# The eight small products of each weight fold at the highest priority on TensorE, in another order

## The chip, the cores and the metric

The kernel runs on one core of one Trainium2 chip. The metric is the device time of one execution in microseconds (us), the median of several runs. Engines are called as in the profile: PE is TensorE (matmuls), PEld its weight loads, DVE is VectorE, ACT ScalarE, POOL GpSimd, SP SyncE, which issues most DMAs. All arithmetic is in 32-bit floats; a matmul of the program whose operands are plain float32 leaves two MATMUL records in the trace, so that eight small products show as x16.

## The reference

Three stages follow each other. The first is attention by landmarks, for 4 batches (b) of 8 heads with 576 tokens of 64 numbers:

```
A = softmax(q k_lm^T);  Bm = softmax(q_lm k_lm^T);  C = softmax(q_lm k^T)
Z = an approximate inverse of Bm, by 6 steps of  Z = 2 Z - Z Bm Z
attn = A Z C v
```

`q_lm` and `k_lm` are means over blocks of 18 tokens, 32 of them per head. The second and third stage are gated feed-forward layers over the 2304 tokens (width 512):

```
x1 = ((attn w_a) * (attn w_b)) w_out          inner width 1536
x2 = (h * tanh(softplus(h))) w_out2,  h = x1 w_in2     inner width 2048
```

## The kernel before, in words

The attention output is never formed. For each batch the small matrix `Z C v` of all heads is kept as a tile `mt` (128x128, `MT[b]`), and the weights `w_a` and `w_b` are multiplied by it in advance: that is a **fold**. `fold(b, g)` (line 558) takes one sixth `g` of the inner width and issues eight products: for each half `c` of the 128 rows (64 rows each) and each of four strips `j` of 32 output partitions, a product of 64 rows by 32 columns with 512 columns streamed. The strips `j` and halves `c` lie on different parts of PE's array; the result fills `ps_bm`, a pair of PSUM banks (`pair_bank("bm")`, line 82, one buffer only). ACT then copies it to a tile `bm` (the high part), and DVE subtracts that from PSUM (the low part); `bm` has three buffers. There are 4 x 6 = 24 folds. They are numbered here 1 to 24 in their order on PE.

Each `ab` step (line 591) multiplies `bm` by the tile `at` of the attention weights, twice six matmuls of 128x128 with 288 columns into `ps_ab`; ACT and DVE make the gated product `g` of it, POOL its low part. `emit_o1` (line 630) multiplies `g` by the second weights into `ps_o`, twelve matmuls at a time, and ACT or DVE evict it to `x2acc`. Beside this run the attention of later batches (tiles `rz`, `bc`, `ET`, `E`, `kt`, `qt`; many small products of 32x32 or 64x32) and the conversion of the 64-bit input weights to float32 (`to_f32`, line 444: a DMA into one of three `stg` buffers, one ACT and four DVE instructions into `f` or `wab`). The folds of batches 0 and 1 use `wab` tiles straight from that conversion; those of batches 2 and 3 load them back from DRAM (`load_wab`, line 519; three `wab` buffers).

What sets the order: up to the end of a list written by hand (`ORDER_1`, issued at line 840) the instructions of PE, ACT and DVE are held in the order in which the program writes them; folds 1 to 4 lie there. From then on a scheduler draws up each engine's order beforehand: of the instructions that its own model of time takes to be ready it puts the one with the highest priority first, and priority otherwise follows the order in which the program wrote them. SP's DMAs are ordered in this way too. On the chip each engine then works through its own list strictly in order and waits by semaphores. The last third of the program (the third stage) is again mostly held.

Of the kernel before, what the change touches and what calls it, by code (L numbers as in the profile page):

```python
# [31 lines left out]
def nystrom_moe_kernel(ctx: ExitStack, tc: tile.TileContext, q, k, v, w_a, w_b, w_out1, w_in2, w_out2, q1, k1, out):  # L32
# [49 lines left out]
    def pair_bank(tag):  # L82
        return two.get(tag, ps).tile([128, 2, 512], F32, tag=tag, bufs=1, name=f"ps_{tag}")
# [473 lines left out]

    def fold(b, g):
        p = pair_bank("bm")
        for c in range(2):  # L560
            r = slice(64 * c, 64 * c + 64)
            for j in range(4):
                pe.matmul(
                    p[32 * j:32 * j + 32, c], MT[b][r, 32 * j:32 * j + 32],
                    wab[g][r, j].rearrange("p a f -> p (a f)"), start=True, stop=True,
                )
        t = main.tile([128, 2, 2, 512], F32R, tag="bm", bufs=3, name="bm")
        yield
        ac.activation(t[:, 0], p, AF.Copy)
        yield  # L570
        ve.tensor_tensor(t[:, 1], p, t[:, 0].bitcast(F32), op=ALU.subtract)
        bm[b, g] = t

    def emit_bm(b, g):
        for _ in fold(b, g):
            pass
# [239 lines left out]
    for n in range(N_UNITS):  # L816
        part[f"c{n}"] = unit(n)
    part["f0"], part["f1"], part["F0"], part["F1"] = fold(0, 0), fold(0, 1), fold(1, 0), fold(1, 1)
    for n in range(N_SLOTS):
        b, m = divmod(n, 8)  # L820
# [343 lines left out]
```

## Time and profile before

| what | value |
|---|---|
| median of 3 runs | 831.23 us (830.99 to 831.99) |
| profiled execution, own time | 834.0 us |
| its span in the trace | 832.2 us |
| PE busy | 797.8 us, 96% of the span |
| DVE busy | 541.7 us, 65% |
| ACT busy | 361.1 us, 43% |
| chain that ended last | PE 78%, DVE 8%, DMA 7%, ACT 3% |

Busy time is the union of an engine's instructions. Matmuls are pipelined and a record is longer than the distance to the next start, so what an instruction or a group costs PE is read as the distance from its start to the next group's start. All folds lie in the first half, between 35 and 405 us.

### The profile page before, as it was taken

To read this page: it belongs to the slowest core of one execution; us is meant where nothing else is said; L and a number is where in the kernel's file an instruction comes from. 1 tells how busy PE (TensorE), PEld (TensorE's weight loads), DVE (VectorE), ACT (ScalarE), POOL (GpSimd) and SP (SyncE) were. 2 spreads that over 40 slices of the span, in tenths; PEclk is the share of its full clock that TensorE was granted. 3 is DMA by queue.
4 is the path that set the end of the run, shared out by engine and by line. 5 is a ranking of instruction groups with operands and counts; after the bars stand their busy time and mean duration, and the time that the engine had idled before them with its cause. 6 is when DMAs were issued, how large, how long until landed. Compare 5 with 4: busy or idle time off the path is not lost.

```text
span 832.2 us, 14803 instructions
## 1 busy us (share of the span) xinstructions
PE 797.8 (96%) x5854; PEld 689.5 (83%) x5854; DVE 541.7 (65%) x1012; ACT 361.1 (43%) x824; POOL 141.9 (17%) x143
## 2 busy tenths in 40 slices
PE   5869999999999999999999999999999999999998
PEld 3356778997787887888889889988999999899997
DVE  7868887895498498886796765768433447433433
ACT  3645845444334344454353543554332335332332
POOL 1011212222141242222221344330000000000000
PEclk9889999999999999999999999999999999999999
DMA  9977466558527748868324887878645545555502
GB/s 353 293 280 257 149 233 219 194 179 285 184 68 250 290 143 300 283 209 292 108 93 133 324 335 276 303 280 344 215 179 237 217 185 232 215 192 224 191 0 76
DMA packets 48732, 183.44 MB, mean 220 GB/s; under 512 B 4260, under 2 KB 12452, under 8 KB 39320
## 3 DMA queue, kind: packets, MB, share of 16 engines
q1 hardware_dynamic: 39832, 169.40, 57.1%
q10 hardware_dynamic: 8832, 13.11, 4.3%
q8 instruction: 46, 0.75, 0.4%
q14 instruction: 22, 0.18, 0.1%
HBM read 129.02 MB, written 53.48 MB: 219 GB/s over the span
## 4 chain that ended last, share of the span: by engine, by line
PE 78%; DVE 8%; DMA 7%; ACT 3%; issue 3%; SPq 1%; ACTq 0%; POOL 0%; DVEq 0%
PE ps_ab L56 35%; PE ps_o L56 22%; PE ps_bm L56 12%; PE ps_at L56 10%; DMA tok<-in_k_dram 2%; DMA kt<-in_k_dram 2%; DVE f L56 2%; DMA vt<-in_v_dram 1%; DMA stg<-in_moe_w_a_dram 1%; DMA stg<-in_moe_w_out_dram 1%; ACT sa L56 1%; DVE wab L56 1%; DVE bm L56 1%; DVE tg L56 1%; DVE s L56 1%
## 5 line engine op out<-in xcount | busy, mean ns | idle before, releaser
L56 PE MATMUL ps_ab<-xc,wc 128*128 128x384 f32 x1008 | 197.1, 336 | 1.2 <-DVE u2s L56 1.0
L56 PE MATMUL ps_ab<-at,bm 128*128 128x288 f32 x1152 | 186.6, 302 | 4.7 <-DVE tg L56 3.5
L56 PEld LDWEIGHTS ps_ab<-xc,wc 128*128 128x128 f32 x1008 | 178.5, 188 | 12.5 <-DVE u2s L56 1.4
L56 PEld LDWEIGHTS ps_ab<-at,bm 128*128 128x128 f32 x1152 | 160.9, 189 | 30.2 <-issue 9.2
L56 PE MATMUL ps_o<-g,wo 128*128 128x288 f32 x1152 | 180.1, 299 | 3.7 <-ACT x2acc L56 3.0
L56 PEld LDWEIGHTS ps_o<-g,wo 128*128 128x128 f32 x1152 | 161.7, 190 | 18.4 <-issue 5.5
L608 POOL TENSOR_TENSOR g<-tg,g 128x288 fp32r<-128x288 f32 x96 | 88.7, 925 | 337.6 <-ACT g L56 274.2
L56 ACT ACTIVATE m<-c 128x384 f32<-128x384 f32 x95 | 49.6, 522 | 176.6 <-DVE c L56 174.5
L56 PE MATMUL ps_bm<-wo,g 128*128 128x512 f32 x288 | 92.8, 391 | 0.0
L56 DVE TENSOR_TENSOR g<-m,g 128x384 fp32r<-128x384 f32 x96 | 62.2, 650 | 30.5 <-ACT g L56 30.0
L56 PE MATMUL ps_at<-wo,g 128*128 128x512 f32 x288 | 81.5, 391 | 0.0
L56 PE MATMUL ps_o<-wo,g 128*128 128x512 f32 x288 | 78.7, 390 | 0.0
L56 DVE SCALAR_TENSOR_TENSOR f<-stg,f 128x512 uint32<-128x512 uint32 x88 | 69.8, 796 | 1.4
L56 ACT ACTIVATE g<-tg 128x288 fp32r<-128x288 f32 x96 | 42.4, 441 | 58.1 <-DVE tg L56 57.4
L56 ACT ACTIVATE ta<-ps_ab 128x288 f32<-128x288 f32 x96 | 38.9, 406 | 63.1 <-PE ps_ab L56 60.1
L56 PEld LDWEIGHTS ps_at<-wo,g 128*128 128x128 f32 x288 | 54.0, 188 | 10.2
L56 DVE TENSOR_TENSOR tg<-ps_ab,ta 128x288 f32<-128x288 f32 x96 | 43.3, 451 | 28.9 <-PE ps_ab L56 22.5
L56 PEld LDWEIGHTS ps_o<-wo,g 128*128 128x128 f32 x288 | 53.6, 188 | 8.7
L56 PEld LDWEIGHTS ps_bm<-wo,g 128*128 128x128 f32 x288 | 53.4, 188 | 6.3
L56 ACT ACTIVATE g<-m 128x384 fp32r<-128x384 f32 x96 | 50.4, 525 | 3.0
L56 DVE TENSOR_TENSOR u2s<-ps_ab,m 128x384 f32<-128x384 f32 x24 | 13.4, 557 | 57.9 <-PE ps_ab L56 57.9
L56 DVE TENSOR_TENSOR c<-ps_ab,m 128x384 f32<-128x384 f32 x23 | 12.8, 558 | 48.6 <-PE ps_ab L56 48.6
(156 smaller groups left out, 803.4 us busy)
## 6 DMA issues: line engine op xcount, KB each, us to landing
wc<-wcd SPq DMA_DIRECT2D x16, 1792.0 KB, 7.4
wo<-wod SPq DMA_DIRECT2D x16, 1024.0 KB, 9.5
stg<-in_moe_w_out_dram SPq DMA_DIRECT2D x28, 512.0 KB, 5.1
wcd<-wc SPq DMA_DIRECT2D x8, 1792.0 KB, 10.6
wab<-wabd SPq DMA_DIRECT2D x10, 1024.0 KB, 7.5
stg<-in_moe_w_in_dram SPq DMA_DIRECT2D x16, 512.0 KB, 6.0
wod<-wo SPq DMA_DIRECT2D x8, 1024.0 KB, 8.4
stg<-in_moe_w_a_dram SPq DMA_DIRECT2D x12, 512.0 KB, 7.4
```

The lines of the kernel that those rows point to most:

```text
L56: i = f(*a, **kw)
L608: gp.tensor_tensor(t[:, 1], tg, t[:, 0].bitcast(F32), op=ALU.subtract)
```

## The change

Inside `fold` the eight products are now traced in a block that gives them the highest priority, and within each half `c` the strips `j` come in the order 3, 2, 1, 0 instead of 0, 1, 2, 3. The products, their operands and their places on the array are the same. The eviction by ACT and DVE keeps its priority.

```
     def fold(b, g):
         p = pair_bank("bm")
-        for c in range(2):
-            r = slice(64 * c, 64 * c + 64)
-            for j in range(4):
+        with tc.high_priority():
+            for c, j in ((c, j) for c in range(2) for j in (3, 2, 1, 0)):
+                r = slice(64 * c, 64 * c + 64)
                 pe.matmul(
                     p[32 * j:32 * j + 32, c], MT[b][r, 32 * j:32 * j + 32],
                     wab[g][r, j].rearrange("p a f -> p (a f)"), start=True, stop=True,
                 )
```

In the order before, 14 folds stand as one group of eight on PE and 10 (folds 5, 6, 9, 11, 12, 17, 18, 21, 23 and 24) in 25 pieces, 39 groups in all; now all 24 stand as one group of eight. Three places of PE's order follow. In them `ps_bm<-wab,mt` are a fold's products, `ps_ab` those of an `ab` step, `ps_o_<n>` those of `emit_o1`, `ps_at<-rz` and `ps_at<-ident,E` small products of the next batch's attention.

The first place, before: fold 11 of batch 1 on PE, at 197 to 208 us of the trace, in four pieces (3, 1, 1 and, behind the rows shown, 3 products).

```order
L56 MATMUL ps_bm<-wab,mt 32x512 x3
L56 MATMUL ps_at<-ident,E 128x128 x4
L56 MATMUL ps_at<-ident,E 64x128
L56 MATMUL ps_bm<-wab,mt 32x512
L56 MATMUL ps_ab<-at,bm 128x288 x12
L56 MATMUL ps_o_2713<-g_2569,wo_2374 128x288
L56 MATMUL ps_o_2758<-g_2459,wo_2181 128x288
L56 MATMUL ps_o_2713<-g_2569,wo_2374 128x288 x2
L56 MATMUL ps_o_2758<-g_2459,wo_2181 128x288 x2
L56 MATMUL ps_o_2758<-g_2526,wo_2181 128x288 x3
L56 MATMUL ps_o_2758<-g_2569,wo_2374 128x288 x3
L56 MATMUL ps_bm<-wab,mt 32x512
```

The same place now, folds 11 and 12:

```order
L56 MATMUL ps_bm<-wab,mt 32x512 x8
L56 MATMUL ps_ab<-at,bm 128x288 x8
L56 MATMUL ps_at<-rz 32x64 x8
L56 MATMUL ps_o_2713<-g_2459,wo_2181 128x288 x3
L56 MATMUL ps_o_2713<-g_2526,wo_2181 128x288 x3
L56 MATMUL ps_o_2758<-g_2459,wo_2181 128x288 x3
L56 MATMUL ps_o_2758<-g_2526,wo_2181 128x288 x3
L56 MATMUL ps_ab<-at,bm 128x288 x6
L56 MATMUL ps_bm<-wab,mt 32x512 x8
L56 MATMUL ps_ab<-at,bm 128x288 x3
```

Fold 11 has moved forward by 22 other matmuls (counted to its first piece) and is whole; fold 12, whose three pieces stood 86 to 176 matmuls behind fold 11's first piece, stands 34 behind fold 11.

The second place, before: fold 18 on PE, at 322 to 326 us of the trace.

```order
L56 MATMUL ps_o_4259<-g_4050,wo_3808 128x288 x3
L56 MATMUL ps_o_4259<-g_4094,wo_3808 128x288 x3
L56 MATMUL ps_bm<-wab,mt 32x512 x5
L56 MATMUL ps_ab<-at,bm 128x288 x6
L56 MATMUL ps_bm<-wab,mt 32x512 x3
L56 MATMUL ps_o_4315<-g_4130,wo_3669 128x288 x3
```

The same place now:

```order
L56 MATMUL ps_o_4259<-g_4050,wo_3808 128x288
L56 MATMUL ps_o_4259<-g_4094,wo_3808 128x288 x2
L56 MATMUL ps_bm<-wab,mt 32x512 x8
L56 MATMUL ps_ab<-at,bm 128x288 x6
L56 MATMUL ps_o_4259<-g_4094,wo_3808 128x288
L56 MATMUL ps_o_4315<-g_4130,wo_3669 128x288 x3
```

Fold 18 stands where its first piece stood; the second piece behind the six products of `ps_ab` is gone.

The third place, before: the matmuls ahead of fold 20 on PE, the last nine rows of the sixty matmuls between folds 19 and 20.

```order
L56 MATMUL ps_o_4405<-g_4275,wo_3808 128x288 x3
L56 MATMUL ps_o_4449<-g_4130,wo_3669 128x288 x3
L56 MATMUL ps_o_4449<-g_4175,wo_3669 128x288 x3
L56 MATMUL ps_o_4449<-g_4231,wo_3808 128x288 x3
L56 MATMUL ps_o_4449<-g_4275,wo_3808 128x288 x3
L56 MATMUL ps_ab<-at,bm 128x288 x12
L56 MATMUL ps_o_4493<-g_4331,wo_3161 128x288 x3
L56 MATMUL ps_o_4493<-g_4375,wo_3161 128x288 x3
L56 MATMUL ps_bm<-wab,mt 32x512 x8
```

The same place now, from fold 19 to fold 20:

```order
L56 MATMUL ps_bm<-wab,mt 32x512 x8
L56 MATMUL ps_ab<-at,bm 128x288 x12
L56 MATMUL ps_o_4315<-g_4275,wo_3808 128x288 x3
L56 MATMUL ps_o_4359<-g_4275,wo_3808 128x288 x3
L56 MATMUL ps_ab<-at,bm 128x288 x6
L56 MATMUL ps_o_4405<-g_4130,wo_3669 128x288 x3
L56 MATMUL ps_o_4405<-g_4175,wo_3669 128x288 x3
L56 MATMUL ps_o_4405<-g_4231,wo_3808 128x288 x3
L56 MATMUL ps_o_4405<-g_4275,wo_3808 128x288 x3
L56 MATMUL ps_bm<-wab,mt 32x512 x8
```

Fold 20 now follows fold 19 after 36 matmuls instead of 60.

Elsewhere the scheduler's order of the other instructions changes too, on PE, DVE, ACT and SP, from about fold 10 on: small products of the attention and `ab` or `emit_o1` groups swap places, and two loads of `wab` on SP's queue (for folds 14 and 15) stand ahead of a load of `stg` and of the next `kt`.

## Rows read from the trace of the kernel before

**Rows 1.** The page: busy time by engine; shares of the chain that ended last.

```profile
PE 797.8 (96%) x5854; PEld 689.5 (83%) x5854; DVE 541.7 (65%) x1012; ACT 361.1 (43%) x824; POOL 141.9 (17%) x143
...
PE 78%; DVE 8%; DMA 7%; ACT 3%; issue 3%; SPq 1%; ACTq 0%; POOL 0%; DVEq 0%
```

**Rows 2.** Groups by line: a fold's products and ACT's eviction (count | busy, mean ns).

```profile
L56 PE MATMUL ps_bm<-wab,mt 64*32 64x512 f32 x384 | 42.0, 608 | 0.2 <-DVE bm L56 0.2
...
L56 ACT ACTIVATE bm<-ps_bm 128x1024 fp32r<-128x1024 f32 x24 | 24.5, 1023 | 19.9 <-PE ps_bm L56 18.7 <-PE ps_ab L56 1.2
```

**Rows 3.** Timeline of PE around fold 10: start, duration, line, tiles, count.

```profile
186.38 0.96 PE L56 MATMUL ps_ab<-at,bm 128*128 128x288 f32 x6
187.17 0.42 PE L56 MATMUL ps_o<-g,wo 128*128 128x288 f32 x2
...
189.32 1.09 PE L56 MATMUL ps_bm<-wab,mt 64*32 64x512 f32 x16
190.34 1.06 PE L56 MATMUL ps_ab<-at,bm 128*128 128x288 f32 x6
```

**Rows 4.** Timeline of PE, a single product of fold 11.

```profile
199.12 1.04 PE L56 MATMUL ps_bm<-wab,mt 64*32 64x512 f32 x2
200.10 1.86 PE L56 MATMUL ps_ab<-at,bm 128*128 128x288 f32 x12
```

**Rows 5.** Timeline of PE, fold 18: the six matmuls between its pieces, and the second piece.

```profile
323.91 1.06 PE L56 MATMUL ps_ab<-at,bm 128*128 128x288 f32 x6
324.91 1.06 PE L56 MATMUL ps_bm<-wab,mt 64*32 64x512 f32 x6
325.89 0.66 PE L56 MATMUL ps_o<-g,wo 128*128 128x288 f32 x3
```

**Rows 6.** Folds alone by stretch: length, PE busy, PEld busy, ACT busy, PEclk, DMA.

```profile
97.00:130.00 33.00, 5.34 (x48) 0.80 (x48) 0.00 (x0) 1.00 0.65 224
130.00:189.00 59.00, 3.21 (x32) 0.49 (x32) 0.00 (x0) 1.00 0.57 190
189.00:225.00 36.00, 8.44 (x48) 1.18 (x48) 0.00 (x0) 1.00 0.67 229
...
310.00:327.00 17.00, 5.29 (x32) 0.74 (x32) 0.00 (x0) 1.00 0.77 266
...
347.00:410.00 63.00, 8.50 (x64) 1.24 (x64) 0.00 (x0) 1.00 0.64 220
```

**Rows 7.** All work by stretch: length, PE, PEld, DVE, ACT, POOL busy, PEclk, DMA.

```profile
130.00:189.00 59.00, 59.00 (x490) 53.94 (x492) 49.55 (x98) 26.95 (x60) 14.96 (x18) 1.00 0.57 190
189.00:225.00 36.00, 36.00 (x394) 26.30 (x387) 17.38 (x42) 12.14 (x27) 7.18 (x8) 1.00 0.67 229
...
310.00:327.00 17.00, 17.00 (x118) 11.99 (x117) 13.83 (x23) 7.31 (x14) 5.39 (x5) 1.00 0.77 266
...
347.00:410.00 63.00, 62.49 (x457) 53.64 (x458) 48.48 (x86) 28.05 (x59) 14.78 (x16) 1.00 0.64 220
```

**Rows 8.** Chain in order of time, 95 to 135 us: its two longest pieces.

```profile
100.64 8.44 DMA stg<-in_moe_w_a_dram
...
117.20 8.28 DMA stg<-in_moe_w_out_dram
```

**Rows 9.** Chain between 327 and 347 us, shares by line.

```profile
by line: DVE f L56 29.1%; issue 18.2%; DVE bm L56 10.3%; ACT f L451 9.2%; DVE f L455 7.3%; DVE x2acc L56 6.0%; DVE tg L56 5.2%; ACTq L620 5.0%; POOL g L608 4.1%; ACT g L56 2.2%; PE ps_ab L56 2.1%; PE ps_o L56 2.0%; DVEq L56 0.2%; DVEq L455 
```

**Rows 10.** Chain between 408 and 425 us, shares by line.

```profile
by line: DVE f L56 22.8%; issue 20.4%; PE ps_ab L56 11.8%; DVE xq L56 10.0%; DVE wc L56 6.0%; DVE tg L56 5.3%; DVE f L455 5.0%; ACT f L451 4.3%; ACT wc L56 3.7%; DVE xc L56 3.3%; DVE bm L56 3.0%; ACT g L56 2.6%; DVE x2acc L56 1.3%; ACTq L62
```

**Rows 11.** What PE's matmuls waited for between 97 and 410 us: total, times, longest.

```profile
PE ps_ab L56 <- DVE tg L56: 1.4, 2, 0.9
PE ps_o L56 <- ACT x2acc L56: 1.2, 1, 1.2
```

**Rows 12.** Timelines of PE and DVE: fold 19 and the end of its eviction.

```profile
330.84 1.09 PE L56 MATMUL ps_bm<-wab,mt 64*32 64x512 f32 x16
...
338.49 1.21 DVE L56 TENSOR_TENSOR bm<-ps_bm,bm 128x1024 fp32r<-128x1024 f32 x1
```

## The prediction

> **What bounds the kernel now.** I read the page first, then the same thing by stretch, because a mean over the span mixes stages. PE's matmuls fill 96% of the span and the chain that ended last is 78% PE [rows 1]. All folds lie before 405 us, so the folds alone by stretch came next [rows 6], then all engines in the same stretches [rows 7], then PE's timeline around single folds [rows 3 to 5], and last who ends PE's waits and where the chain leaves PE [rows 8 to 11]. The reader is to see three things. First, a fold is tiny work that takes real PE time: 42.0 us in all [rows 2]. Second, its price goes by the group and not by the product (next part). Third, PE has hardly a wait between 97 and 410 us: the two longest entries are 1.4 and 1.2 us [rows 11]. In the stretches from 130 to 225 us PE's row is full while DVE is busy 49.55 of 59 us and then only 17.38 of 36 [rows 7]. There PE time that goes is time that goes. In two places it is not so. Between 97 and 130 us the chain sits in two weight loads of 8.44 and 8.28 us [rows 8], half of that stretch. Between 327 and 347 us [rows 9], and again between 408 and 425 us [rows 10], it runs through DVE's and ACT's conversion of weights (`f`), with PE at a few per cent of it in the first case. PE's granted clock is at its upper level (1.00) in all these stretches [rows 6, 7], and since the work is the same I leave the clock out.
>
> **The change, part by part.**
>
> *The pieces that go.* A whole fold, eight products, costs PE 190.34 - 189.32 = 1.02 us from its start to the next group's [rows 3]. One product alone costs 200.10 - 199.12 = 0.98 us [rows 4], three cost 325.89 - 324.91 = 0.98 us [rows 5]. The eight evidently run side by side, and a piece pays for a whole fold. Ten folds stand in 25 pieces and now stand in 10: 15 pieces go. Beside this each group of small products costs at its turns: six `ab` matmuls take 187.17 - 186.38 = 0.79 us among their like [rows 3] and 324.91 - 323.91 = 1.00 us between two pieces [rows 5], so 0.21 us for the two turns. A piece that goes gives back its 0.98 us, less some 0.01 by which the piece that takes over its products grows (1.02 for eight against 0.98 for one to three), and 0.2 for its turns: about 1.17 us, and 15 of them 17.5 us.
>
> As a check, by busy time [rows 6]: the five stretches hold 5.34 + 3.21 + 8.44 + 5.29 + 8.50 = 30.8 us for 14 folds (3, 2, 3, 2 and 4 of them). At 1.09 us [rows 3] for each, whole, they would hold 15.3, so 15.5 us go; 0.06 us per piece of this overlaps the next group (1.04 against 0.98 [rows 4]), 0.9 in all, and with 15 x 0.2 for the turns it is 17.6 again.
>
> *What comes back.* The order now puts fold 10 inside a group of 32x32 products, splits a group of landmark products in two, and a pair of `zd` products likewise. No row shows these; by the nearest rows each costs between nothing and a piece with its turns (1.17). I take about a third, 1.0 us for the three together, and keep 0 to 3.5 for the range.
>
> *What of it is on the path, by stretch.* The pieces that go are 2, 1, 5, 3 and 4 in the five stretches (from the orders; [rows 6] agree).
> - 97 to 130 us, 2 pieces, 2.3 us: nothing. The two loads [rows 8] start when DVE has emptied a staging buffer, and PE already waits behind them. PE only waits longer.
> - 130 to 189, 1 piece, 1.2 us: DVE is at 49.55 of 59 us. I take half, 0.6.
> - 189 to 225, 5 pieces, 5.8 us less the 1.0 that comes back: 4.8. DVE is half idle, the path is PE, and what follows moves forward as a whole. The two `wab` loads that move ahead of `kt` on SP wait for folds 11 and 12, which now come earlier, so they do not hold the queue longer.
> - 310 to 327, 3 pieces, 3.5 us: directly behind them the chain is DVE's [rows 9]. DVE is busy 13.83 of 17 us [rows 7], so it can follow by 3.2 at the very most. I take 1.0.
> - 347 to 410, 4 pieces, 4.7 us: DVE is at 48.48 of 63 us and PE is the path, but at its end the chain goes over to DVE and ACT [rows 10]. I take 3.0.
>
> The sum is 0 + 0.6 + 4.8 + 1.0 + 3.0 = 9.4 us. What is late next in each case is DVE, with the conversion of the second weights.
>
> *The start order 3, 2, 1, 0* changes no cost: the eight run together in 1.02 us. Bounds: nothing, to a few start distances per fold, (1.02 - 0.98) x 24 = 1.0 us.
>
> *The eviction* (ACT 1023 ns [rows 2], then DVE 1.21 us [rows 12]) is the same 24 times; it moves with its fold.
>
> Against the profiled execution: 834.0 (span 832.2 and 1.8 around it) - 9.4 = 824.6 us. That execution is 2.8 us over the median of 831.23, so in medians 831.2 - 9.4 = **822 us**.
>
> **A rule weighed.** In the stretch 189 to 225 us PE's matmul row is full, its weight loads fill 26.30 of 36 us, in the stretch before 53.94 of 59 [rows 7]. The Trainium skill (Perfetto Trace Analysis, Identifying the Most-Contended Engine) says that matmul busy time is a poor measure of PE's headroom and that weight-load busy time is to be taken. By it the stretch could be packed to the same 91%, 26.30 / 0.914 = 28.8 us, an estimate of 7.2 us saved where I count 4.8. The trace bears out the direction (the folds hold 8.44 us of matmuls there and 1.18 us of weight loads [rows 6]), but the three whole folds that stay need 3.3 us, so I keep my figure.
>
> **The rivals.**
>
> *All of it arrives.* If DVE and ACT follow PE in every stretch after 130 us, 13 x 1.17 - 1.0 = 14.2 us go: 817. For it: DVE's idle time in the stretches 310 to 327 and 347 to 410 us is 17.7 us [rows 7]. Against: the chain there [rows 9, 10].
>
> *Nothing arrives.* The gain is a longer wait of PE for DVE's conversions: 831. For it: DVE at 84% in 130 to 189 and 81% in 310 to 327 [rows 7], and a new order of everything else that may cost the rest. Against: the five pieces in 189 to 225 us, where DVE has half its time free.
>
> *Slower: a fold at the head of PE's list that waits for its bank.* There is one `ps_bm`, and a fold can start when DVE has evicted the one before. Fold 20 now comes 36 matmuls after fold 19, 36 x 0.79 / 6 = 4.7 us, and with two turns 4.9. In the trace before, fold 19 ended at 330.84 + 1.02 = 331.86 and its eviction at 338.49 + 1.21 = 339.70, 7.8 us later [rows 12]; at that pace PE would stand 2.9 us at fold 20, with everything behind it. Folds 11, 12 and 19 (37, 34 and 31 matmuls after the one before) stand as close. If all four wait 2.9 us and no other gain is lost, 9.4 - 11.6 = -2.2: 833.4. It decides from 9.4 / 4 = 2.4 us of wait at each, that is evictions that end some 7 us after their fold. Against: with ACT and DVE free, an eviction needs 2.2 us, and in 189 to 225 they are mostly free.
> The Trainium skill (TensorE: Matmul & The Clock Gate, Part 2, Step-by-step) says that matmuls stay in program order and only weight loads are pulled ahead, so such a fold would indeed hold all matmuls behind it. No row before shows a long case of it.
>
> **How the numbers follow.** Forecast (part of it arrives, 818 to 828): 0.62. All of it (814 to 818): 0.17. Nothing (829.6 to 832.9): 0.09. Slower (833 to 837): 0.12. A measurement of this kernel can tell 0.2%, 1.7 us, from no change. So faster is 0.62 + 0.17 and a little of the third case's lower edge, 0.80; same 0.08; slower 0.12. The range that holds eight in ten reaches from 814 (all 17.5 us, the first stretch's too) to 831 (nothing); the likeliest case's own range is 818 to 828.
>
> **What would show it.** 24 rows of a fold in PE's timeline, all x16, and PE busy for folds near 24 x 1.09 = 26 us in place of 42.0: the first step. The six `ab` matmuls beside folds near 0.9. By stretch: PE reaches the 12th fold's place some 5 us earlier and the distance holds to fold 16; between the 17th and the 20th fold it hardly grows; PE's waits between 97 and 410 us grow: the two entries of 2.6 us together [rows 11] become 7 us or more, most of it for DVE. The prediction is wrong if `PE ps_bm <- DVE bm` becomes a wait of several us (slower), if waits do not rise (all of it), or if a fold of eight costs clearly more than 1.02 us.

## The result, and the profile after

The changed kernel takes 819.41 us (median of 4 runs, 818.69 to 821.62); the kernel before took 831.25 us beside it (830.99 to 831.99). The ratio is 0.9858 with an interval of 0.9839 to 0.9876, so 11.8 us went. A second comparison of the same two kernels, on another occasion, gave 818.71 against 832.71 us: 0.9829 (0.9806 to 0.9852), 14.0 us. Beside e1 to e3 below, two executions of the kernel before took 1543 and 2680 us; times and ratios there go by its other executions, whose median is 832.2 us. The profiled execution of the changed kernel took 819.76 us with a span of 818.0.

The page of the changed kernel, busy time by engine and the shares of the chain that ended last, answers to [rows 1]:

```profile
PE 779.9 (95%) x5854; PEld 686.8 (84%) x5854; DVE 541.6 (66%) x1012; ACT 359.5 (44%) x824; POOL 139.1 (17%) x143
...
PE 79%; DVE 9%; DMA 5%; ACT 4%; issue 2%; POOL 0%; ACTq 0%; SPq 0%; DVEq 0%
```

The work is the same (5854 matmuls, DVE's busy time alike), and PE is busy 797.8 - 779.9 = 17.9 us less. The groups by line of the changed kernel (count | busy, mean ns) answer to [rows 2]:

```profile
L56 PE MATMUL ps_bm<-wab,mt 64*32 64x512 f32 x384 | 26.1, 600 | 0.5 <-DVE bm L56 0.5
```

42.0 us of busy time for folds became 26.1. PE's timeline of the changed kernel around folds 11 and 12 (start, duration, line, tiles, count), which answers to [rows 3, 4]:

```profile
194.11 1.09 PE L56 MATMUL ps_bm<-wab,mt 64*32 64x512 f32 x16
195.13 1.34 PE L56 MATMUL ps_ab<-at,bm 128*128 128x288 f32 x8
...
199.32 1.09 PE L56 MATMUL ps_bm<-wab,mt 64*32 64x512 f32 x16
```

Every fold is one row of x16, and takes 195.13 - 194.11 = 1.02 us to the next start, what a whole fold took before.

Where the time came from is read between two landmarks, since the time up to fold 7 differs from execution to execution by some 3 us (fold 7 starts between 121.8 and 125.3 us in all profiles of this study but e8's, where it starts at 130.4). One cause shows in the two profiles of the changed kernel: fold 5 starts at 100.75 and 100.74 us, but between 109 and 112.4 us, right behind a wait of PE of about 2 us in both, the granted clock was 0.67 on average in the first and stayed at its upper level, 1.00, in the second, and fold 7 starts 1.9 us later in the first. The landmarks are the start of fold 7 and the first product of the third stage. From the second landmark to the last product of that kind it is 374.4 us in both kernels: the third stage neither gained nor lost. The view of one tile has it for the kernel before (count: shortest/median/longest ns, first to last start; form):

```profile
L56 PE MATMUL ps_ab<-xc,wc x1008: 331/336/445, 446.9 to 821.3; 128*128 128x384 f32 x168
```

and for the changed kernel:

```profile
L56 PE MATMUL ps_ab<-xc,wc x1008: 331/336/444, 432.7 to 807.1; 128*128 128x384 f32 x168
```

Fold 7 itself in PE's timeline, before:

```profile
124.55 1.09 PE L56 MATMUL ps_bm<-wab,mt 64*32 64x512 f32 x16 [0.17 <-DVE bm L56]
```

and after:

```profile
124.54 1.09 PE L56 MATMUL ps_bm<-wab,mt 64*32 64x512 f32 x16 [0.47 <-DVE bm L56]
```

The distance fell from 446.9 - 124.55 = 322.3 to 308.1 us, by 14.2. Two further executions give 321.4 for the kernel before and 309.0 for the changed one. By sections, against the second execution of the kernel before, and with a fold in several pieces taken at the start of its last piece: fold 7 to 9 (one piece less) -1.2 us, 9 to 10 +0.1, 10 to 13 (five pieces) -4.3, 13 to 16 +0.1, 16 to 17 -2.3, 17 to the third stage -5.6 (these last two hold seven pieces): -13.3. Fold 7 itself hardly came earlier, though two pieces had gone ahead of it: it starts at 124.55 and 123.22 us in the two profiles before and at 124.54 and 122.61 after.

How much of this is PE's own work is read in the windows view between the two landmarks (length, PE, PEld, DVE, ACT, POOL busy, PEclk, DMA). Before:

```profile
124.55:446.86 322.31, 317.29 (x2806) 272.35 (x2807) 247.72 (x476) 141.91 (x302) 83.50 (x90) 1.00 0.60 207
```

and after:

```profile
124.54:432.68 308.14, 303.58 (x2806) 270.72 (x2807) 246.88 (x476) 140.81 (x302) 79.88 (x90) 1.00 0.61 212
```

PE is busy 317.29 - 303.58 = 13.7 us less, and stands idle 5.0 us before and 4.6 after. All that PE saved here is time saved.

What lets 310 to 410 us shrink is seen in the same view, taken over windows that hold as many instructions. Before:

```profile
310.00:410.00 100.00, 99.14 (x733) 82.98 (x732) 78.65 (x137) 43.18 (x89) 25.09 (x26) 1.00 0.72 246
```

After:

```profile
303.00:395.00 92.00, 90.65 (x732) 81.50 (x731) 78.13 (x137) 42.22 (x89) 23.63 (x27) 1.00 0.76 259
```

137 DVE instructions and 733 (732) matmuls take 92 us in place of 100; the granted clock is 1.00 in both. DVE is busy 85% in place of 79%. What DVE waited for on PE's account in these two windows (total, times, longest), before:

```profile
DVE tg L56 <- PE ps_ab L56: 6.9, 8, 1.7
DVE xt L56 <- PE ps_bm L56: 2.3, 1, 2.3
DVE x2acc L56 <- PE ps_o L56: 1.5, 2, 1.3
```

and after:

```profile
DVE tg L56 <- PE ps_ab L56: 3.3, 5, 1.3
DVE tg L56 <- PE ps_o L56: 1.4, 1, 1.4
```

Before, DVE stood 6.9 + 2.3 + 1.5 = 10.7 us waiting for PE; after, 4.7. So DVE, which the prediction had as the next limit here, was itself kept waiting by PE.

The chain needs a second execution to be read. In the first profile of the kernel before it is 29.1% DVE's `f` between 327 and 347 us [rows 9]. In the second profile of the same kernel (b_again below) fold 19 stands 1.7 us earlier, and the shares by line at the same place, 325 to 345 us, are all PE's:

```profile
by line: PE ps_o L56 46.0%; PE ps_ab L56 44.7%; PE ps_bm L56 10.2%
```

Two paths of nearly the same length evidently lie side by side there, and [rows 9] shows the one that came last by a little in one execution. In the changed kernel the chain at this place is mostly PE's too. Its shares by line between 320 and 345 us:

```profile
by line: PE ps_ab L56 40.6%; PE ps_o L56 33.9%; DVE f L56 9.3%; PE ps_bm L56 4.1%; ACT bm L56 4.1%; issue 3.5%; DVE f L455 1.5%; ACTq L620 1.4%; ACT ta L56 1.2%; ACT f L451 0.3%; DVE tg L56 0.3%; ACTq L451 0.1%
```

Between 408 and 425 us the chain is DVE's in both profiles of the kernel before ([rows 10], and 28.0% `f` in the second). There it did turn to PE. Its shares between 394 and 411 us, after:

```profile
by line: PE ps_ab L56 45.5%; PE ps_o L56 22.6%; DVE f L56 10.2%; issue 9.8%; ACT wc L56 5.4%; ACT ta L56 4.3%; ACTq L620 1.9%; DVE x2acc L56 0.4%; DVE tg L56 0.4%; DVEq L56 0.3%; ACT f L451 0.2%; ACTq L451 0.1%; ACTq L56 0.1%
```

### The profile page after: what moved, and what is told of

Read it like the earlier page. It is cut to its first block, busy times and chain, and to the rows that moved or that the text cites. A ratio compares the mean times of both kernels' runs of the same rounds, so it can differ in the third digit from the quotient of the medians.

```text
span 818.0 us, 14799 instructions
## 1 busy us (share of the span) xinstructions
PE 779.9 (95%) x5854; PEld 686.8 (84%) x5854; DVE 541.6 (66%) x1012; ACT 359.5 (44%) x824; POOL 139.1 (17%) x143
## 4 chain that ended last, share of the span: by engine, by line
PE 79%; DVE 9%; DMA 5%; ACT 4%; issue 2%; POOL 0%; ACTq 0%; SPq 0%; DVEq 0%
PE ps_ab L56 36%; PE ps_o L56 23%; PE ps_at L56 10%; PE ps_bm L56 10%; DMA kt<-in_k_dram 2%; DVE f L56 2%; ACT sa L56 1%; DVE wab L56 1%; DMA stg<-in_moe_w_a_dram 1%; DMA stg<-in_moe_w_out_dram 1%; DVE bm L56 1%; DVE s L56 1%; DMA s_in<-wi2d 1%; DVE xt L56 1%; DVE f L455 0%
## 5 line engine op out<-in xcount | busy, mean ns | idle before, releaser
L608 POOL TENSOR_TENSOR g<-tg,g 128x288 fp32r<-128x288 f32 x96 | 86.5, 901 | 325.7 <-ACT g L56 314.4
```

The lines of the kernel that those rows point to most:

```text
L608: gp.tensor_tensor(t[:, 1], tg, t[:, 0].bitcast(F32), op=ALU.subtract)
```

## The experiments

Ratios are to the kernel before, run beside each. "Distance" is that from fold 7 to the third stage in the run's own profile.

| run | time (us) | ratio (interval) | groups of fold products | distance (us) |
|---|---|---|---|---|
| before / b_again | 831.25 / 831.66 (one run) | 1 | 39 | 322.3 / 321.4 |
| the change / c_after_again | 819.41 / 818.71 | 0.9858 / 0.9829 | 24 | 308.1 / 309.0 |
| e1_only_5_6 | 832.33 | 1.0000 (0.9988 to 1.0012) | 37 | 322.2 |
| e2_only_9_12 | 827.07 | 0.9938 (0.9918 to 0.9958) | 33 | 315.9 |
| e3_only_17_24 | 823.95 | 0.9903 (0.9886 to 0.9921) | 32 | 314.1 |
| e4_not_5_6 | 818.36 | 0.9831 (0.9807 to 0.9854) | 26 | 307.3 |
| e5_priority_alone | 825.52 | 0.9912 (0.9890 to 0.9934) | 27 | 312.3 |
| e6_order_alone | 825.90 | 0.9930 (0.9909 to 0.9950) | 30 | 315.4 |
| e7_extra_first | 824.17 | 0.9893 (0.9869 to 0.9917) | 24 + 24 | 313.3 |
| e8_extra_between | 845.63 | 1.0137 (1.0099 to 1.0176) | 48 + 24 | 328.8 |
| e9_evict_too | 820.93 | 0.9850 (0.9830 to 0.9871) | 24 | 309.3 |
| e10_landmarks_too | 817.60 | 0.9816 (0.9799 to 0.9833) | 24 | 307.3 |

**A second look at the kernel before** (no edit):

> The kernel before, unchanged, profiled a second time, because its first profiled execution (834.0 us) lay 2.8 us over its median. Theory A (the early stretch, bound by weight loads, varies from execution to execution): this one ends near 831.2 us, and fold 7 starts about 2.5 us earlier than the 124.55 us of the first, while from fold 7 to the end nothing differs by more than 0.5 us. Rival B: the 2.8 us are spread over the whole span, and fold 7 starts within 0.8 us of 124.55.

831.66 us; fold 7 stood at 123.22 us in place of 124.55, and the distance was 0.9 us shorter. Neither theory holds as stated: of the 2.3 us by which the span is shorter, 1.3 lie ahead of fold 7 and 0.9 behind it. This last is the size below which a difference between two profiles says nothing here.

**The change for some folds only** (e1 to e4). The folds are counted as the program writes them; those in `FIRST` get the change, the others stay as before:

```
-        with tc.high_priority():
-            for c, j in ((c, j) for c in range(2) for j in (3, 2, 1, 0)):
+        folds[0] += 1
+        with tc.high_priority() if folds[0] in FIRST else nullcontext():
+            for c, j in ((c, j) for c in range(2) for j in ((3, 2, 1, 0) if folds[0] in FIRST else (0, 1, 2, 3))):
```

e1, `FIRST = (5, 6)`, the two pieces between 97 and 130 us:

> Only folds 5 and 6 are made whole (2 pieces go, between 97 and 130 us); the order of DVE, POOL and SP is that of the kernel before. My theory (that stretch is bound by two weight loads, PE only waits longer): no change, 831.2 us within 0.7. Rival (a piece is worth its 1.17 us of PE time wherever it stands): 828.9 us.

832.33 us against 832.2. Folds 5 and 6 stand whole, and the time does not move: the interval of 1.0000 is 1.0 us to either side, and the rival asked for 2.3. Two pieces there are worth nothing that can be told.

e2, `FIRST = range(9, 13)`, the six pieces between 130 and 225 us:

> Only folds 9 to 12 are whole (6 pieces go, between 150 and 225 us). Prediction's credits: 0.6 + 4.8 = 5.4 us, so 825.8. If every piece after 130 us arrives at 1.17 us: 7.0 less up to 1.0 for split groups of other products, 824.2 to 825.2. If the gain came from the new order of everything else in the later part and not from these pieces: 830 to 831.5.

0.62% of 832.2 is 5.2 us, with an interval of 3.5 to 6.8; the distance fell by 5.5 to 6.4. That rules out the third case, but not one of the first two.

e3, `FIRST = range(17, 25)`, the seven pieces between 310 and 410 us:

> Only folds 17 to 24 are whole (7 pieces go, between 310 and 405 us). Prediction's credits: 1.0 + 3.0 = 4.0 us, so 827.2, because DVE's weight conversion takes over as the bound there. If every piece arrives at 1.17 us: 8.2 us, so 823.0. In the profile the first would show waits of PE for DVE or ACT between 310 and 425 us grow by about 4 us, the second would show them the same.

0.97% of 832.2 is 8.1 us, with an interval of 6.6 to 9.5; the distance fell by 7.3 to 8.2. Seven pieces at 1.17 are 8.2, and the 4.0 of the prediction's credits is ruled out. PE's waits for DVE and ACT between 310 and 425 us are 2.0 us here against 1.2 before: they hardly grew, as the second case asks. Together e2 and e3 give 13.3 us, what the sections of the profile give too, so the two parts add up.

e4, all folds but 5 and 6:

> The changed kernel with folds 5 and 6 in two pieces each as before; all else stands as in the changed kernel. My theory (the stretch from 97 to 130 us is bound by two weight loads): as the changed kernel, 819.4 us within 0.8. Rival (a piece costs 1.17 us anywhere): 821.7 us.

818.36 us, 0.2 us below the range of the theory and 3.3 below the rival; the ratio is 0.9831 against 0.9858 and 0.9829 for the whole change. It is the counterpart of e1.

**Priority alone** (e5), the strips in their old order:

```
-            for c, j in ((c, j) for c in range(2) for j in (3, 2, 1, 0)):
+            for c, j in ((c, j) for c in range(2) for j in (0, 1, 2, 3)):
```

> The priority alone, with strips in the order 0, 1, 2, 3: folds 5, 6 and 9 stand in two pieces, all others whole (27 groups; the change has 24, before 39). If groups set the time and those before 130 us are free: one piece more than the changed kernel, 819.4 + 1.2 = 820.6 us. If the order of strips itself mattered to PE: a fold of eight would take clearly more or less than 1.02 us from its start to the next group.

A miss, by some 5 us: 825.52. Only folds 5, 6 and 9 are split, so one extra piece stands on the path, yet the distance is 312.3, 4.2 us over the change's, and the third stage is 1.8 us longer (435.9 to 812.1, 376.2 us). The scheduler's order of everything else is another. What PE waited for between 300 and 470 us, in this run (total, times, longest):

```profile
PE ps_ab L56 <- DVE tg L56: 2.9, 5, 1.0
PE ps_bm L56 <- DVE g L56: 1.4, 1, 1.4
PE ps_o L56 <- ACT g L56: 0.9, 1, 0.9
PE ps_o L56 <- DVE x2acc L56: 0.7, 2, 0.5
```

and in the changed kernel:

```profile
PE ps_ab L56 <- ACT ta L56: 2.5, 4, 1.4
PE ps_o L56 <- POOL g L608: 0.4, 1, 0.4
```

These are 5.9 us against 2.9, so about 3 of the 5 us are seen as waits of another order; the one of 1.4 us for `g` lies in the third stage. PE's own work is the other part: between the landmarks it is busy 305.96 us against 303.58 in the change, 2.4 us more, of which the one split has 1.1 to 1.2 by e6. Why the order of the strips leads to that order of the rest was not settled.

**Order alone** (e6), no priority:

```
-        with tc.high_priority():
+        if True:
```

> The order of strips alone (3, 2, 1, 0), without the priority: 30 groups, of which 6 are extra pieces and all of these lie after 130 us. If the number of groups after 130 us sets the time: 819.4 + 6 x 1.17 = 826.4 us, or less by what was lost in the last stretches (prediction's credits: 823 to 825). If the early place of a fold (its priority), not its being whole, gave the gain: 829 to 832 us.

A hit: 825.90, and an early place alone is ruled out as the cause of the gain, since 5.8 us of it came without the priority. Six pieces more than in the change stand behind 130 us, and the distance is 6.4 to 7.3 us over the change's, 1.1 to 1.2 a piece.

**The price of splitting a group, by itself** (e7 and e8). Each fold gets one more product, 128x128 with 32 columns, whose result is not used. In e7 it stands ahead of the eight, in e8 between the first four and the last four:

```
+                if (c, j) == (0, 3):      # e7; in e8: (1, 3)
+                    pe.matmul(p[:, 1, 0:32], ident, ident[:, 0:32], start=True, stop=True)
```

> The changed kernel with one more small product per fold, 128x128 with 32 columns, ahead of the eight, into a part of the bank that they overwrite (a product without use). Folds stay whole. By the nearest rows such a product costs PE about 0.1 us, 24 of them 2.4 us at most: 819.4 to 822 us.

> The same extra product, but between the first four and the last four products of each fold, so that every fold is two pieces (48 groups) with everything else as in the run before it. If a piece costs its own 0.97 us and 0.2 us for turns: 17 folds lie after 130 us, so 17 x 1.17 = 19.9 us more than with the extra product ahead, 839 to 842 us. If the gain came from the folds' early place or the new order of the rest, and pieces were nearly free: within 3 us of it.

PE's timeline of e7, the extra product and the fold behind it:

```profile
193.78 0.30 PE L56 MATMUL ps_bm<-ident 128*128 128x32 f32 x2
194.01 1.09 PE L56 MATMUL ps_bm<-wab,mt 64*32 64x512 f32 x16
```

and of e8:

```profile
196.66 1.06 PE L56 MATMUL ps_bm<-wab,mt 64*32 64x512 f32 x8
197.65 0.41 PE L56 MATMUL ps_bm<-ident 128*128 128x32 f32 x2
197.99 1.06 PE L56 MATMUL ps_bm<-wab,mt 64*32 64x512 f32 x8
198.98 0.26 PE L56 MATMUL ps_at<-bc 32*32 32x32 f32 x6
```

Same instructions, another place: four products take 197.65 - 196.66 = 0.99 us, the other four 0.99 us, where the eight together took 1.02. The kernels differ by 1.0137 - 0.9893 = 2.44% of 833.41, 20.3 us for 24 more groups. That splitting alone costs time is shown by this: the rival allowed 3 us.

The size is another matter. The expectation reached nearly this sum, 19.9 us, by 17 folds behind 130 us alone; the time itself, 845.63, lies above its 839 to 842. The windows view between the landmarks, where 18 folds lie, counted from fold 7, has for e7:

```profile
121.77:435.05 313.28, 305.90 (x2841) 275.03 (x2841) 246.98 (x476) 140.53 (x302) 83.09 (x90) 1.00 0.61 213
```

and for e8:

```profile
130.36:459.18 328.82, 326.05 (x2843) 278.35 (x2843) 248.45 (x476) 141.57 (x302) 81.97 (x90) 1.00 0.58 203
```

PE's busy time grew by 326.05 - 305.90 = 20.2 us, 1.12 for each of 18 splits, close to the 1.17 foretold; but PE's idle time fell from 7.4 to 2.8 us, so only 15.5 us arrived, 0.86 each. The rest of the difference of the two profiles lies ahead of fold 7, which starts 8.6 us later in e8, and is in part the clock. Between 64 and 76 us the granted clock was 1.00 in e7 and at its lower level in e8, where PE had been busy 0.88 of the 2 us from 60 to 62:

```profile
64.00:76.00 12.00, 12.00 (x102) 7.11 (x94) 5.98 (x13) 3.32 (x8) 0.00 (x0) 0.50 0.62 226
```

Folds 3 to 6 then stand 6.9 to 7.2 us later than in e7, so the splits between them cost next to nothing there, as in e1. That the total came near 17 x 1.17 is luck.

e7 itself came out above its expectation of 822 at most: 24 times the extra product's 0.23 us is 5.5, and 0.9893 is 0.35% or 0.64% over the change's two ratios, 2.9 or 5.3 us. The scheduler's order is not the change's throughout: fold 17 starts 178.1 us after fold 7 in e7, 183.7 in the change, and at folds 5, 6, 9 and 17 other matmuls stand between the extra product and the eight. So this is no clean price of the product.

**The eviction too** (e9): ACT's and DVE's instruction of a fold also at the highest priority.

```
-        ac.activation(t[:, 0], p, AF.Copy)
+        with tc.high_priority():
+            ac.activation(t[:, 0], p, AF.Copy)
```

(and the same for DVE's subtraction)

> The changed kernel with the two evictions of each fold (ACT and DVE) at the highest priority as well. If PE still waits for evictions here and there: 0.5 to 1.5 us faster, 818 to 819. If DVE's time is only moved from other work: no change, 819.4 within 1. If the evictions push the weight conversion back where the chain runs through it: 820 to 822.

0.9850, between the two comparisons of the change (the kernel before stood at 833.41 beside it, so 820.93 itself says less). PE's wait at fold 7 stayed 0.47 us, and a wait for ACT ahead of fold 20 (1.35 us in the change, see below) stayed 1.30. An earlier place for the eviction buys nothing that can be told.

**The landmark products too** (e10): the eight small products of each `tile4` group, the landmark products, get the same block.

```
-            for c in range(2):
-                for j in range(4):
+            with tc.high_priority():
+                for c in range(2):
+                    for j in range(4):
```

> The changed kernel with the other groups of eight small products (landmark products of the attention, 64x32) at the highest priority as well, so that none of them is split. One group in the changed order is split in two: 1 piece of about 0.5 us and 0.2 for turns, so 818.7 us; no change that a run can tell is as likely.

817.60 us, 0.9816: surely faster than the kernel before, and at most a little faster than the change, since the interval overlaps that of the change's second comparison, though not that of the first. Where it differs is read in PE's timeline. In the changed kernel, between folds 9 and 10:

```profile
174.80 1.06 PE L56 MATMUL ps_ab<-at,bm 128*128 128x288 f32 x6
175.78 0.68 PE L56 MATMUL ps_bm<-kt,ql 64*32 64x288 f32 x4
176.39 1.85 PE L56 MATMUL ps_o<-g,wo 128*128 128x288 f32 x12
```

and in e10, the same place:

```profile
173.03 1.07 PE L56 MATMUL ps_ab<-at,bm 128*128 128x288 f32 x6
173.94 1.23 PE L56 MATMUL ps_o<-g,wo 128*128 128x288 f32 x8
```

The last two landmark products of this group, which stood apart in the kernel before as well, are back with the others. Their piece took 176.39 - 175.78 = 0.61 us and the six `ab` matmuls ahead of it 0.98 in place of 0.91, and the section from fold 9 to 10 takes 31.30 us where the change takes 32.14: 0.8 us less. In the medians it can't be told apart. The group that the change itself had split, at 228 us, is still split in e10, so its expectation that none would be did not hold.

**The change once more**:

> The changed kernel once more, for the size of its gain: in the profiles of five kernels so far the distance from fold 7 to the first product of the third stage is 321.4 to 322.3 us with 13 extra pieces and 307.3 to 308.1 with none, 13 to 14 us, while the medians of its first runs differ by 11.8 us. If the difference is the start (fold 7 began at 124.5 us in its first profile, at 122.4 to 124.8 in others): fold 7 to the third stage again 308 us within 0.5, and a ratio to the kernel before of 0.983 to 0.986. If the first runs were right and the profiles not typical: 0.986 and a distance of 309 to 310 us.

818.71 us. The ratio, 0.9829, is that of the first theory within its rounding, but the distance of 309.0 is that of the second: neither holds whole. With this the change's own two comparisons, 11.8 and 14.0 us, enclose the 13.3 of e2 and e3.

## Why the prediction was right, point by point

The time, 819.4 against 822.0, lies in the likeliest case's range, and the mechanism is the one that was named: a fold's price goes by the group. Two terms of the sum were too small. That the time fell into this range and not into that of the rival is in part luck: 0.9829, the second comparison, would make it 817.0.

*A piece costs a whole fold: right.* Foretold were about 26 us of busy time for folds and 17.5 us of PE time in all; it is 26.1, and PE's busy time fell by 17.9. Between the landmarks 13 x 1.17 - 1.0 = 14.2 us of PE's time were due and 13.7 are measured. e8 shows the cause by itself.

*The turns, 0.2 us for two: right.* Six `ab` matmuls beside a fold should take near 0.9. PE's timeline of the changed kernel, behind fold 18, and at folds 19 and 20:

```profile
315.88 1.06 PE L56 MATMUL ps_ab<-at,bm 128*128 128x288 f32 x6
316.78 0.95 PE L56 MATMUL ps_o<-g,wo 128*128 128x288 f32 x6
...
320.35 1.09 PE L56 MATMUL ps_bm<-wab,mt 64*32 64x512 f32 x16
321.37 1.86 PE L56 MATMUL ps_ab<-at,bm 128*128 128x288 f32 x12
...
325.39 1.06 PE L56 MATMUL ps_ab<-at,bm 128*128 128x288 f32 x6 [1.35 <-ACT ta L56]
...
327.99 1.09 PE L56 MATMUL ps_bm<-wab,mt 64*32 64x512 f32 x16
```

316.78 - 315.88 = 0.90 us.

*What comes back, 1.0 us: a little small, 1.5.* The landmark group that the change splits, in PE's timeline after:

```profile
228.01 0.68 PE L56 MATMUL ps_bm<-kt,ql 64*32 64x288 f32 x4
228.61 1.06 PE L56 MATMUL ps_ab<-at,bm 128*128 128x288 f32 x6
229.61 0.70 PE L56 MATMUL ps_bm<-kt,ql 64*32 64x288 f32 x12
```

The first piece takes 0.60 us and the six matmuls 1.00 in place of 0.79 among their like, 0.8 us together, the price by the group again. In the same timelines the group of 32x32 products around fold 10 takes 0.33 us in two parts in place of 0.17, and the `zd` pair at 304.59 us takes 0.72 in two parts in place of 0.36 and makes the one matmul between them 0.2 longer. That is 0.8 + 0.16 + 0.56, some 1.5 us in all. None of the three was undone by itself.

*97 to 130 us, nothing: right*, by e1 and e4. The chain there still holds the two loads of [rows 8]. In order of time, after:

```profile
98.98 8.90 DMA stg<-in_moe_w_a_dram
...
117.49 8.00 DMA stg<-in_moe_w_out_dram
```

*130 to 225 us, 0.6 + 4.8 = 5.4: right*, with 5.2 (3.5 to 6.8) in e2. Half of the piece between 130 and 189 us was given away because DVE was at 84%; by the profile all 1.2 us came.

*The rule weighed.* The estimate of 7.2 us for 189 to 225 us was too high: the three folds there came 4.3 us closer by the profile. The windows view, after:

```profile
188.00:220.00 32.00, 32.00 (x404) 27.15 (x393) 19.24 (x44) 12.45 (x29) 7.54 (x9) 1.00 0.78 288
```

Weight loads now fill 27.15 of 32 us, 85%, and not 91%, with every fold whole. The direction of the Trainium skill's rule (Perfetto Trace Analysis, Identifying the Most-Contended Engine) holds, as PE's row is as full as before and 4 us shorter; how far it goes was better read from the groups.

*310 to 327 us, 1.0 of 3.5, and 347 to 410, 3.0 of 4.7: the steps that failed.* Their 4.0 us measured 8.1 (e3). The step said that the chain behind the pieces is DVE's, so that DVE can follow only in part. Two things were wrong in it. It read the path from one execution: in the second one of the same kernel the chain behind fold 18 is PE's. And it took DVE's busy share for a limit of its own, where DVE had 10.7 us in that stretch in which it waited for PE; these waits fell to 4.7, and DVE did the same work in 8 us less. At the stretch's end, where the chain was DVE's in both executions, it turned to PE. So of the rivals "all of it arrives" (14.2 us) describes 130 us and later better than the forecast does; that the first comparison came to 11.8 and the second to 14.0 is the spread between comparisons.

*PE's waits grow from 2.6 to 7 us or more, mostly for DVE: wrong.* PE's waits between 97 and 400 us, after, which answer to [rows 11]:

```profile
PE ps_o L56 <- ACT x2acc L56: 2.0, 1, 2.0
PE ps_ab L56 <- ACT ta L56: 1.9, 3, 1.4
PE ps_ab L56 <- DVE tg L56: 0.9, 1, 0.9
PE ps_bm L56 <- DVE bm L56: 0.5, 1, 0.5
```

The two kinds that were 2.6 us are 2.9, and the wait of 2.0 us lies at 108.91 us, in the stretch where nothing was credited. All entries together went from 4.1 us (97 to 410 us, before) to 5.6; what grew most behind 130 us is PE's wait for ACT's `ta`, not for DVE. The sign "if waits do not rise, all of it arrives" was the one that came nearest. By place, the lead was to hold to fold 16, which it does; it was hardly to grow between folds 17 and 20, but grew by 4.0 us, in part because fold 20 now stands earlier among the other matmuls.

*The fold that waits for its bank: did not come, but by little.* Fold 20, the last row of the timeline above, starts without a wait of its own, 6.6 us after the end of fold 19 and not 4.9. The row at 325.39 us is why: PE stood 1.35 us there for ACT's `ta`, in an order in which ACT had first to copy fold 19 (from 324.02 to 325.03 us). The second profile has the same wait, 1.39. Fold 20's bank came free 1.45 us before it, by DVE's timeline:

```profile
325.32 1.22 DVE L56 TENSOR_TENSOR bm<-ps_bm,bm 128x1024 fp32r<-128x1024 f32 x1
```

The eviction ended at 326.54, 5.2 us after fold 19's end at 321.37 and not 7.8 as in [rows 12]. Without the 1.35 us the bank would have been free only some 0.1 us ahead of the fold. The only wait for the bank is fold 7's 0.47 us. The rival decided from 7 us, and its 2.9 us a fold would have needed evictions as late as before.

*The start order of the strips changes no cost: half right.* A fold costs 1.02 us in either order. But the order of the eight decides where the scheduler puts them, and all the rest: e5 lost some 5 us against the count of its pieces, e6 gained 5.8 (0.70% of 832.5) from the order alone. The prediction counted the strips' start distances and not this; the sum was saved because it was made on the order that both parts give.

## What to carry to other kernels

Small products that run side by side on parts of PE's array cost by the group: count the groups in PE's timeline, not the products, and take the distance from start to start of a group of one and of a whole group for the price of splitting. Before a saving on PE is discounted because the chain runs through another engine, look at the chain of a second execution of the same kernel, and at that engine's own waits in the same stretch: those for PE are what it can give back. And where a scheduler orders the program, price a small edit by the whole order that it makes, since the priority without the order of the strips was worth some 5 us less than the count of its pieces said.

## What the runs showed that was not expected

One extra product of 128x128 with 32 columns ahead of a fold costs 0.23 us (194.01 - 193.78), and in the middle of one 0.34 us (197.99 - 197.65) plus the second group's 0.99. The expectation had put it at about 0.1; what makes up the rest was not separated by a run. And a split costs PE 1.12 us of busy time in e8, but only 0.86 us of the distance, because PE's idle time there shrank by 4.6 us.
